# Moving 128 rows of the second dense matrix to 64 partitions, and splitting the bias, x and last output-weight transfers

## The chip, the core and the metric

The kernel runs on one core of a Trainium2 chip. A time is the device time of one execution in microseconds (us); the figure for a kernel is the median over several executions. Beside it there is one profiled execution, taken by the hardware profiler, with a time of its own.

## The reference, cut to what matters

There are two batch rows of one token each, with 448 features. A layer norm of x feeds two branches, and the output is x plus both.

```python
xn = _layernorm(x)                       # x: [2, 1, 448], bf16
# branch A: decode attention, 16 query heads on 8 key/value heads, head size 256
q = (xn @ wq)                            # wq: [448, 4096]
k, v = last 4096 positions of k_cache, v_cache   # [2, 8, 32768, 256]
p = softmax(q k^T / 16)
a = (p v) @ wo                           # wo: [4096, 448]
# branch B: a dense layer, an activation, a dense layer
h = xn @ w1 + b1                         # w1: [448, 1792], b1: [1792]
act = h * tanh(log1p(exp(h)))            # "mish"
b = act @ w2                             # w2: [1792, 448]
out = x + a + b
```

The keys and values that are read come to 67 MB; wq and wo are 3.7 MB each, w1 and w2 are 1.6 MB each. All of it is read once.

## The kernel before, in words

The order of every engine's instructions is the order of the program text (`tc.manual_schedule()`); the framework adds the waits. All large loads are issued by SyncE (SP) on one hardware queue, and ScalarE (ACT) issues x and the bias on another. Every DMA is cut over the core's 16 DMA engines, and each of these works through its own share of the queue in order.

Large loads go into a ring of three buffers (`kv`, bufs=3) of 32 KB per partition. In order of the program these are: K of step 0 first half (L98), wq (L132), K second half, w1 (L502), and then, for each step u, K of the next step, V of this step, K second half, V second half (L106), and the output weights `wo` of the step (L113). In the last step V comes in pieces, the output weights in two transfers (L119), and w2 in four parts (L556). A load waits until the buffer's earlier contents have been used. A DMA's completion is counted on one of eight semaphores, given out in turn to the DMAs of both queues, so that a DMA is also not issued before the one eight places earlier has landed.

The 8 key/value heads are worked on in four steps u of two heads each. In a step VectorE (DVE) transposes K in SBUF (`turns`, L271, two instructions for each half), TensorE (PE) computes the scores (`scores`, L358), ACT takes the exponential (L366), DVE transposes the result into `p` (L369) and swaps parts of it (L338 to L340), PE sums the weights (`weigh`, L382) and multiplies them with V (`values`, L404). `gather` (L416, L422), `finish` (L449) and `relay` (L463, L474) bring the head outputs into shape, and `mix_early` (L483) multiplies them with `wo` into one PSUM tile, `early`, which holds x from the start (L231). In the last step `carry` moves `early` to the accumulator `acc` (L238, L240), and `values_fixed` (L437), `mix` and `dense_out` (both through `add_rows`, L251) add to `acc`; DVE and ACT copy `acc` to the result (L619, L621), and SP stores it (L622).

Branch B: `dense_in` (L513) computes h for the 1792 hidden features with 49 matmuls as soon as w1 is there, `mish` (L527 to L545, with the bias from L128) turns it into `act_bf`, both in step 0. `dense_out` multiplies it with w2 at the very end. The hidden features are held as two halves k of 896; in each half, partition p has the seven features 7p to 7p+6, and so row 7p+i of the half of w2 lies on partition p at place i:

```python
w2_parts = ((0, 0, NI), (1, 0, 4), (1, 4, 6), (1, 6, NI))   # half, first place, last place; NI = 7
```

Of the kernel before, what the change touches and what calls it, by code (L numbers as in the profile page):

```python
# [11 lines left out]
BF16 = mybir.dt.bfloat16  # L12
FP32 = mybir.dt.float32
# [4 lines left out]
def kernel(  # L18
# [13 lines left out]
    nc = tc.nc  # L32
    P = 128
# [5 lines left out]
    Bsz, Sq, D = A_x.shape  # L39
    _, Hkv, Sk, Dh = A_k_cache.shape  # L40
    HqDh = A_wq.shape[1]
    Hq = HqDh // Dh
    rep = Hq // Hkv
# [4 lines left out]
    U = Hkv // KU  # L48
# [9 lines left out]
    NS = 7  # L58
    HW = HqDh // 2
    NCH = HW // P  # L60
    F2 = F // 2
    NI = F2 // P
# [6 lines left out]

    lead_pool = ctx.enter_context(tc.tile_pool(name="lead", bufs=1))  # L70
    lead_pool.tile([P, 192], BF16, name="lead")
    kv_pool = ctx.enter_context(tc.tile_pool(name="kv", bufs=3))
    kt_pool = ctx.enter_context(tc.tile_pool(name="kt", bufs=1))
    wo_pool = ctx.enter_context(tc.tile_pool(name="wo", bufs=2))
    p_pool = ctx.enter_context(tc.tile_pool(name="pp", bufs=1))
    consts = ctx.enter_context(tc.tile_pool(name="consts", bufs=1))
# [7 lines left out]
    ps_m = ctx.enter_context(tc.tile_pool(name="ps_m", bufs=1, space=PSUM))  # L84
# [5 lines left out]
    def ring(name):  # L90
        return kv_pool.tile([P, RK * KE], BF16, tag="kv", name=name)
# [3 lines left out]
    def load_k(u, r):  # L95
        t = ring("k")
        src = kview[u][:, s0:, :].rearrange("j (c t) d -> c j (t d)", c=C)
        nc.sync.dma_start(out=t[:], in_=src[:, :, r * RK * KE : (r + 1) * RK * KE])  # L98
        k_t[u, r] = t

    def load_v(u, g, lo=0, hi=TV):
        if lo == 0:
            v_t[u, g] = ring("v")
        t = v_t[u, g]
        src = vview[u][:, s0:, :].rearrange("j (g x t) d -> g x j (t d)", g=GV, x=C)
        nc.sync.dma_start(  # L106
            out=t[:, lo * Dh : hi * Dh], in_=src[g, :, :, lo * Dh : hi * Dh]
        )

    def load_wo(u):  # L110
        w = wo_pool.tile([P, KU, rep, 2 * D], BF16, tag="wo", name="wo")
        if u < U - 1:
            nc.sync.dma_start(  # L113
                out=w[:].rearrange("p k h e -> p (k h e)"),
                in_=A_wo.rearrange("(k u y i) d -> u y k (i d)", k=KU, u=U, i=8)[u],
            )
        for k2 in range(KU if u == U - 1 else 0):
            r0 = (u + U * k2) * rep * Dh
            nc.sync.dma_start(  # L119
                out=w[:, k2, :, :],  # L120
                in_=A_wo[r0 : r0 + rep * Dh, :].rearrange("(h p c) d -> p h (c d)", h=rep, p=P),
            )
        wo_t[u] = w

    x_bf = consts.tile([Bsz, D], BF16)
    nc.scalar.dma_start(out=x_bf[:, :], in_=A_x.flatten_outer_dims())
    b1_sb = consts.tile([P, 2, NI], BF16)
    nc.scalar.dma_start(out=b1_sb[:], in_=B_b1.rearrange("(k q c) -> q k c", k=2, q=P))  # L128

    load_k(0, 0)  # L130
    wq = ring("wq")
# [1 line left out]
        out=wq[:, 0 : NS * HW], in_=A_wq.flatten().rearrange("(p e) -> p e", p=P)  # L133
# [4 lines left out]
    ident = consts.tile([P, P], BF16)  # L138
# [9 lines left out]
    for k in range(KU):  # L148
        nc.gpsimd.tensor_copy(
            out=hot[:, k, :, :, :, k],  # L150
            in_=ident[:].rearrange("p (q y) -> p y q", y=4).unsqueeze(2)
            .to_broadcast([P, 4, rep, 32]),
        )
    eps_t = consts.tile([Bsz, 1], FP32)
    nc.vector.memset(eps_t[:], 1e-5)
# [7 lines left out]
        out=rstd[:], in_=mv[:, 1:2], func=ACT.Sqrt, bias=eps_t[:], scale=1.0  # L163
# [4 lines left out]
        out=xn_bf[:],  # L168
# [8 lines left out]
        out=parm[:], in_=ident[:].rearrange("p (a o) -> p o a", o=2), axis=AXIS.X, op=ALU.add  # L177
# [3 lines left out]
        out=jm[:],  # L181
        in_=ident[:].rearrange("p (a j h) -> p j a h", j=J, h=rep),
# [4 lines left out]
        out=jm[:], in0=jm[:], scalar1=-1.0, scalar2=29952.0, op0=ALU.add, op1=ALU.mult  # L187
# [3 lines left out]
        out=mneg[:], in_=jm[:].unsqueeze(1).to_broadcast([P, TH * 8, J])  # L191
    )
    sel = consts.tile([P, 2, NQ], FP32)
    for x in range(2):
        for w in range(4):
            at = 32 * w + (2 * (w % 2) + x) * NQ
            src = ident[:, at : at + NQ]
            if w == 0:
                nc.vector.tensor_copy(out=sel[:, x, :], in_=src)
            else:  # L200
                nc.vector.tensor_tensor(
                    out=sel[:, x, :], in0=sel[:, x, :], in1=src, op=ALU.add
# [16 lines left out]
    for odd in range(2):  # L219
        for half in range(2):  # L220
            o = (half + odd) % 2
            nc.vector.tensor_scalar(
                out=xs[:, odd::2, half * Bsz : (half + 1) * Bsz],
# [6 lines left out]
    early = ps_e.tile([Bsz, D], FP32)  # L230
# [18 lines left out]
    def add_rows(lhsT, rows, stop=False):  # L249
        for g in range(G):  # L250
            nc.tensor.matmul(  # L251
                acc[32 * g : 32 * g + Bsz, :],
                lhsT=lhsT,
                rhs=rows[:, g * DG : (g + 1) * DG],
                start=False,
                stop=stop,
                skip_group_check=True,
            )
# [9 lines left out]
    def turns(u, i):  # L268
        t = k_t.pop((u, i))
        for r in range(RK):  # L270
            nc.vector.transpose(  # L271
                out=kt[i][:, :, r, :, :],
                in_=t[:, r * KE : (r + 1) * KE].bitcast(FP32).rearrange(
                    "p (a c j) -> p a c j", c=P // (R * J), j=J
                ),
            )

    spread = {}
    for n in range(2):
        for e in range(2):  # L280
# [3 lines left out]
                out=sp[:],  # L284
                in_=ident[:, o : o + 63 : 2].unsqueeze(1).to_broadcast([P, G, 32]),
# [91 lines left out]
    state = {}  # L377

    def weigh(u):
        dn = ps_den.tile([P, G * TH, NQ], FP32, tag="dn", name="dn")  # L380
        for i in range(NH):
            nc.tensor.matmul(  # L382
                dn[:].rearrange("p a q -> p (a q)"),
                lhsT=ones[:],
                rhs=p_run[:, i].rearrange("p t q -> p (t q)"),
                start=(i == 0),
                stop=(i == NH - 1),
            )
        rec = small.tile([P, NQ], FP32, tag="rec", name="rec")
        nc.vector.tensor_reduce(  # L390
            out=rec[:], in_=dn[:].rearrange("p a q -> p q a"), axis=AXIS.X, op=ALU.add
        )
        nc.vector.reciprocal(out=rec[:], in_=rec[:])
        state["rec", u] = rec
# [84 lines left out]
    def mix_early(u):  # L479
        ox = state.pop(("ox", u))  # L480
        w = wo_t.pop(u)[:].rearrange("p k h (c d) -> p (k h c) d", c=2)
        for i in range(8):
            nc.tensor.matmul(  # L483
                early[:],
                lhsT=ox[:, i, :],
                rhs=w[:, i, :],
                start=False,
                stop=(u == U - 2 and i == 7),
            )
# [8 lines left out]
    act_bf = consts.tile([P, NI, 2, Bsz], BF16)  # L498

    def load_w1():  # L500
        t = ring("w1")
        nc.sync.dma_start(  # L502
            out=t[:, 0 : NS * F2], in_=B_w1.flatten().rearrange("(p e) -> p e", p=P)
        )
        state["w1"] = t

    def dense_in():
        w1 = state.pop("w1")
        w1_v = w1[:, 0 : NS * F2].rearrange("p (s q i) -> p s i q", s=NS, i=NI)
        h_ps = ps_m.tile([P, NI, 2, Bsz], FP32, tag="m", name="h_ps")  # L510
        for i in range(NI):
            for s in range(NS):
                nc.tensor.matmul(  # L513
                    h_ps[:, i, :, :].rearrange("p k b -> p (k b)"),
                    lhsT=w1_v[:, s, i, :],
                    rhs=xs[:, s, 0 : 2 * Bsz],
                    start=(s == 0),
                    stop=(s == NS - 1),
                    skip_group_check=True,
                )  # L520
        state["h"] = h_ps
# [23 lines left out]
        nc.vector.tensor_tensor(out=act_bf[:], in0=h_sb[:], in1=t_sb[:], op=ALU.mult)  # L545

    KH = 4096
    w2_parts = ((0, 0, NI), (1, 0, 4), (1, 4, 6), (1, 6, NI))

    def load_w2(part):  # L550
        if part == 0:
            state["w2"] = ring("w2")
        k, lo, hi = w2_parts[part]
        w2_in = B_w2.flatten().rearrange("(k p e) -> k p e", k=2, p=P)
        at = k * KH
        nc.sync.dma_start(  # L556
            out=state["w2"][:, at + lo * D : at + hi * D],
            in_=w2_in[k, :, lo * D : hi * D],
        )

    def dense_out(part):
        k, lo, hi = w2_parts[part]
        for i in range(lo, hi):
            at = k * KH + i * D
            add_rows(
                act_bf[:, i, k, :], state["w2"][:, at : at + D], stop=(k == 1 and i == NI - 1)
            )

    load_w1()
    turns(0, 0)  # L570
    project()
    scores(0, 0)
# [2 lines left out]
    mish()  # L575
    scores(0, 1)
    weigh(0)
    for u in range(U - 1):
        load_k(u + 1, 0)
        load_v(u, 0)  # L580
        load_k(u + 1, 1)
        load_v(u, 1)
        load_wo(u)
        turns(u + 1, 0)
        values(u, 0)
        scores(u + 1, 0)
        turns(u + 1, 1)
        values(u, 1)
        gather(u)
        finish(u)  # L590
        scores(u + 1, 1)
        weigh(u + 1)
        relay(u)
        mix_early(u)
    u = U - 1
# [19 lines left out]
    for g in range(G):  # L615
        dst = res[:, g * DG : (g + 1) * DG]
        src = acc[32 * g : 32 * g + Bsz, :]
# [35 lines left out]
```

## Time and profile before

| | |
|---|---|
| median of 6 runs | 189.43 us (189.29 to 189.69) |
| profiled execution, its own time | 190.85 us |
| its span, first to last instruction | 189.1 us |
| PE busy | 85.0 us (45%), 845 matmuls |
| DVE busy | 93.0 us (49%) |
| ACT busy, POOL busy | 12.8 us (7%), 4.7 us (2%) |
| DMA | 77.78 MB in 4719 packets, 411 GB/s over the span |
| mean granted PE clock | 0.667 |

A row of the profile gives the engine, the source line (L271 is line 271 of the kernel), the operation, the tile written and the tiles read, and how often it ran. "PE" is a matmul and "PEld" the load of its weights. A row that begins with SPq or ACTq is the issue of a DMA by that engine's sequencer, not the transfer. "Waits" name the engine and line that waited, and what ended the wait. The "chain that ended last" is followed backwards from the last instruction, at each step to what released it; a DMA in it counts from issue to landing, the time in the queue included.

### The profile page before, as it was taken

How to read it: one execution, taken by the hardware profiler on the slowest of the kernel's cores; microseconds unless marked ns; L12 is line 12 of the kernel's file. 1: busy time of each engine (PE TensorE's matmuls, PEld its weight loads, DVE VectorE, ACT ScalarE, POOL GpSimd, SP SyncE). 2: the span in 40 equal slices, each digit the busy share in tenths (PEclk: the TensorE clock that was granted, in tenths of full speed). 3: DMA queues.
4: the chain of work that ended last, by engine and by line, in shares of the span. 5: the costliest groups of instructions: out<-in, count | busy, mean ns of one | idle time of the engine just before them, and what ended most of it. 6: DMA issues, size and time to landing. Idle time of an engine off the chain costs nothing.

```text
span 189.1 us, 1937 instructions
## 1 busy us (share of the span) xinstructions
PE 85.0 (45%) x845; PEld 36.7 (19%) x849; DVE 93.0 (49%) x93; ACT 12.8 (7%) x26; POOL 4.7 (2%) x16
## 2 busy tenths in 40 slices
PE   0300357563129001892656004874383007838874
PEld 0100112520013000441122001412021002503363
DVE  6729634974891197005990493017960890041001
ACT  3000031001000100101001000110001000110111
POOL 8100000000000000000000000000000000000000
PEclk9999996755556955555578855555769755555585
DMA  5999999999999989999999999999999999999970
GB/s 222 444 416 407 446 437 408 444 440 444 444 444 444 413 383 456 417 430 430 437 444 433 444 444 416 444 444 437 419 402 430 430 416 444 444 419 401 421 318 1
DMA packets 4719, 77.78 MB, mean 411 GB/s; under 512 B 740, under 2 KB 1512, under 8 KB 2280
## 3 DMA queue, kind: packets, MB, share of 16 engines
q1 hardware_dynamic: 4436, 77.66, 96.0%
q8 instruction: 6, 0.10, 0.2%
q10 hardware_dynamic: 276, 0.01, 0.1%
q14 instruction: 1, 0.01, 0.0%
HBM read 77.67 MB, written 0.00 MB: 411 GB/s over the span
## 4 chain that ended last, share of the span: by engine, by line
DMA 43%; PE 25%; DVE 22%; issue 3%; ACT 3%; another core or an unknown queue 1%; SPq 1%; DVEq 0%; ACTq 0%
DMA v<-in_A_v_cache_dram 27%; DVE kt L271 16%; DMA k<-in_A_k_cache_dram 16%; PE pv L404 8%; PE sc L358 8%; PE o L422 4%; DVE p L369 3%; PE early L483 2%; ACT ex L366 1%; ACT vs L416 1%; PE acc L251 1%; DVE rec L390 1%; PE o L437 1%; PE dn L382 1%
## 5 line engine op out<-in xcount | busy, mean ns | idle before, releaser
L271 DVE STREAM_TRANSPOSE kt<-k 128x4096 f32<-128x4096 f32 x16 | 70.0, 4415 | 30.0 <-DMA k<-in_A_k_cache_dram 30.0
L404 PE MATMUL pv<-v,p 128*32 128x512 bf16 x240 | 25.0, 591 | 56.0 <-DMA v<-in_A_v_cache_dram 56.0
L358 PE MATMUL sc<-kt,qd 128*32 128x512 bf16 x256 | 24.6, 537 | 3.3 <-DVE qd L326 1.6
L404 PEld LDWEIGHTS <-p 128*32 128x32 bf16 x240 | 8.9, 133 | 70.5 <-issue 60.7
L449 DVE TENSOR_TENSOR oT<-o,rec 128x16 bf16<-128x16 f32 x4 | 0.7, 175 | 33.0 <-PE o L422 21.2
L369 DVE STREAM_TRANSPOSE p<-ex 128x512 bf16<-128x512 bf16 x8 | 5.2, 690 | 15.9 <-ACT ex L366 15.9
L358 PEld LDWEIGHTS <-qd 128*32 128x32 bf16 x256 | 7.8, 120 | 17.0 <-issue 13.3
L483 PE MATMUL early<-wo,ox 128*2 128x448 bf16 x24 | 9.4, 572 | 1.3 <-ACT ox L474 1.3
L366 ACT ACTIVATE ex<-sc 128x512 bf16<-128x512 f32 x8 | 4.8, 597 | 68.9 <-PE sc L358 43.9
L293 PE MATMUL q_ps<-wq,xs 128*32 128x512 bf16 x28 | 3.2, 629 | 13.3 <-DMA wq<-in_A_wq_dram 13.3
L382 PE MATMUL dn<-p,ones 128*128 128x512 bf16 x5 | 2.8, 607 | 12.0 <-DVE p L340 12.0
L422 PE MATMUL o<-sel,vs 128*128 128x8 f32 x32 | 6.7, 339 | 2.8 <-ACT vs L416 2.8
L422 PEld LDWEIGHTS o<-sel,vs 128*128 128x128 f32 x32 | 6.4, 293 | 6.0 <-ACT vs L416 6.0
L416 ACT COPY vs<-pv 128x512 f32<-128x512 f32 x4 | 2.3, 586 | 54.8 <-PE pv L404 54.8
L390 DVE TENSOR_REDUCE rec<-dn 128x8 f32<-128x512 f32 x4 | 2.8, 692 | 4.5 <-remote 3.4
L214 PE MATMUL xr_ps<-ident,xrows 2*128 2x2 bf16 x7 | 1.0, 181 | 7.2 <-DVE xrows L213 7.2
L513 PE MATMUL h_ps<-xs,w 128*128 128x4 bf16 x49 | 2.8, 193 | 2.7 <-DMA w<-in_B_w_dram 2.7
L293 PEld LDWEIGHTS <-xs 128*32 128x32 bf16 x28 | 1.1, 136 | 14.9 <-issue 14.9
L347 PE MATMUL sc<-mneg,ident 128*128 128x512 bf16 x7 | 3.9, 563 | 0.0
L483 PEld LDWEIGHTS <-ox 128*2 128x2 bf16 x24 | 2.5, 115 | 6.0 <-issue 4.4
L382 PEld LDWEIGHTS <-ones 128*128 128x128 bf16 x8 | 0.6, 110 | 15.5 <-DVE p L340 11.7
L513 PEld LDWEIGHTS <-w 128*128 128x128 bf16 x49 | 2.7, 154 | 3.6 <-DMA w<-in_B_w_dram 3.6
(65 smaller groups left out, 42.4 us busy)
## 6 DMA issues: line engine op xcount, KB each, us to landing
k<-in_A_k_cache_dram SPq DMA_DIRECT2D x8, 4096.0 KB, 27.5
v<-in_A_v_cache_dram SPq DMA_DIRECT2D x7, 4096.0 KB, 19.9
wq<-in_A_wq_dram SPq DMA_DIRECT2D x1, 3584.0 KB, 20.3
wo<-in_A_wo_dram SPq DMA_DIRECT2D x3, 896.0 KB, 18.8
v<-in_A_v_cache_dram SPq DMA_DIRECT2D x1, 2048.0 KB, 17.7
w<-in_B_w_dram SPq DMA_DIRECT2D x1, 1568.0 KB, 13.1
v<-in_A_v_cache_dram SPq DMA_DIRECT2D x1, 1536.0 KB, 21.8
wo<-in_A_wo_dram SPq DMA_DIRECT2D x2, 448.0 KB
```

What stands on the lines that cost most here:

```text
L271: nc.vector.transpose(out=kt[i][:, :, r, :, :], in_=t[:, r * KE : (r + 1) * KE].bitcast(FP32).rearrange("p (a c j) -> p a c j", c=P // (R ...
L293: nc.tensor.matmul(q_ps[32 * u : 32 * (u + 1), :], lhsT=xs[:, s, :], rhs=wq_t[s][:, u * 512 : (u + 1) * 512], start=(s == 0), stop=(s == N ...
L358: nc.tensor.matmul(sc[32 * w : 32 * (w + 1)].rearrange("p t c m -> p t (c m)"), lhsT=qd[:, u, 2 * n + e, :, :].rearrange("p g q -> p (g q) ...
L366: nc.scalar.activation(out=ex[:, :, :, i, :], in_=sc[:], func=ACT.Exp, scale=scale)
L369: nc.vector.transpose(out=p_all[:, :, h * TH : (h + 1) * TH, :].rearrange("p g t q -> p t g q"), in_=ex[:, h * TH : (h + 1) * TH].rearrang ...
L382: nc.tensor.matmul(dn[:].rearrange("p a q -> p (a q)"), lhsT=ones[:], rhs=p_run[:, i].rearrange("p t q -> p (t q)"), start=(i == 0), stop= ...
L390: nc.vector.tensor_reduce(out=rec[:], in_=dn[:].rearrange("p a q -> p q a"), axis=AXIS.X, op=ALU.add)
L404: nc.tensor.matmul(pv[32 * w : 32 * (w + 1), :, :].rearrange("p x d -> p (x d)"), lhsT=p_run[:, g, 4 * a : 4 * a + 4, :].rearrange("p t q ...
L416: nc.scalar.copy(out=sb[:].rearrange("p x d -> p (x d)"), in_=pv[:].rearrange("p x d -> p (x d)"))
L422: nc.tensor.matmul(po[:, c, :], lhsT=sb[:, x, c::2], rhs=sel[:, x, :], start=(x == 0 and c == 0), stop=(last and x == 1), skip_group_check ...
L483: nc.tensor.matmul(early[:], lhsT=ox[:, i, :], rhs=w[:, i, :], start=False, stop=(u == U - 2 and i == 7),)
L513: nc.tensor.matmul(h_ps[:, i, :, :].rearrange("p k b -> p (k b)"), lhsT=w1_v[:, s, i, :], rhs=xs[:, s, 0 : 2 * Bsz], start=(s == 0), stop= ...
```

## The change

**w2.** In each half, the first 128 features are now one to a partition (place 0), and the other 768 are six to a partition (places 1 to 6). `dense_in` takes its weight columns accordingly. Place 0 of the second half, 128 rows of w2, is not in the ring any more: it has a tile of its own, `w2_low`, on partitions 0 to 63 with two rows each, filled by two transfers of 32 partitions right after w1. For it, `dense_out_low` brings the 128 activations into the order of these 64 partitions with two small matmuls (by `perm`, made on POOL) and a copy on DVE, and then adds two matmuls of 448 columns to `early`, in step 0 behind `weigh(0)`. `dense_out` at the end has 13 places in place of 14, in another order of parts.

**Transfers.** The bias comes in four transfers in place of one, x in two, and the output weights of the last step in four in place of two. A pad tile `lead2` is added.

```diff
+    w2_low = lead_pool.tile([P // 2, 2, D], BF16, name="w2_low")
+    lead_pool.tile([P, 128], BF16, name="lead2")
...
         for k2 in range(KU if u == U - 1 else 0):
-            r0 = (u + U * k2) * rep * Dh
-            nc.sync.dma_start(
-                out=w[:, k2, :, :],
-                in_=A_wo[r0 : r0 + rep * Dh, :].rearrange("(h p c) d -> p h (c d)", h=rep, p=P),
-            )
+            for h in range(rep):
+                r0 = ((u + U * k2) * rep + h) * Dh
+                nc.sync.dma_start(
+                    out=w[:, k2, h, :],
+                    in_=A_wo[r0 : r0 + Dh, :].rearrange("(p c) d -> p (c d)", p=P),
+                )
...
-    nc.scalar.dma_start(out=x_bf[:, :], in_=A_x.flatten_outer_dims())
+    for b in range(Bsz):
+        nc.scalar.dma_start(out=x_bf[b : b + 1, :], in_=A_x.flatten_outer_dims()[b : b + 1, :])
     b1_sb = consts.tile([P, 2, NI], BF16)
-    nc.scalar.dma_start(out=b1_sb[:], in_=B_b1.rearrange("(k q c) -> q k c", k=2, q=P))
+    b1_in = B_b1.rearrange("(k f) -> k f", k=2)
+    b1_top = b1_in[:, 0:P].rearrange("k (q c) -> q k c", c=1)
+    b1_low = b1_in[:, P:].rearrange("k (q c) -> q k c", q=P)
+    nc.scalar.dma_start(out=b1_sb[:, :, 0:1], in_=b1_top)
+    for lo, hi in ((0, 48), (48, 96), (96, P)):
+        nc.scalar.dma_start(out=b1_sb[lo:hi, :, 1:NI], in_=b1_low[lo:hi])
...
+    perm = consts.tile([P, 2, 2, 8, 4], BF16)
+    for j in range(2):
+        nc.gpsimd.tensor_copy(
+            out=perm[:, j],
+            in_=ident[:, j::2].rearrange("p (z b a) -> p z a b", z=2, b=4),
+        )
...
-        w1_v = w1[:, 0 : NS * F2].rearrange("p (s q i) -> p s i q", s=NS, i=NI)
+        w1_v = w1[:, 0 : NS * F2].rearrange("p (s f) -> p s f", s=NS)
...
-                    lhsT=w1_v[:, s, i, :],
+                    lhsT=w1_v[:, s, 0:P] if i == 0 else w1_v[:, s, P + i - 1 :: NI - 1],
...
-    w2_parts = ((0, 0, NI), (1, 0, 4), (1, 4, 6), (1, 6, NI))
+    w2_parts = ((0, 1, NI), (1, 1, 5), (1, 5, NI), (0, 0, 1))
+    def w2_at(k, i):
+        return k * KH + (i - 1) * D if i > 0 else 2 * KH
+
+    act_low = consts.tile([P // 2, 2, Bsz], BF16)
+
+    def load_w2_low():
+        rows = B_w2[F2 : F2 + P, :].rearrange("(z b a j) d -> z a b (j d)", z=2, b=4, a=8)
+        for z in range(2):
+            nc.sync.dma_start(
+                out=w2_low[32 * z : 32 * (z + 1)].rearrange("p j d -> p (j d)"), in_=rows[z]
+            )
+
+    def dense_out_low():
+        ap_ps = ps_m.tile([P // 2, 2, Bsz], FP32, tag="m", name="ap_ps")
+        for j in range(2):
+            nc.tensor.matmul(
+                ap_ps[:, j, :],
+                lhsT=perm[:, j].rearrange("p z a b -> p (z a b)"),
+                rhs=act_bf[:, 0, 1, :],
+                start=(j == 0),
+                stop=(j == 1),
+                skip_group_check=True,
+            )
+        nc.vector.tensor_copy(out=act_low[:], in_=ap_ps[:])
+        for j in range(2):
+            nc.tensor.matmul(
+                early[:], lhsT=act_low[:, j, :], rhs=w2_low[:, j, :], start=False, stop=False
+            )
 
     def load_w2(part):
         if part == 0:
             state["w2"] = ring("w2")
         k, lo, hi = w2_parts[part]
-        w2_in = B_w2.flatten().rearrange("(k p e) -> k p e", k=2, p=P)
-        at = k * KH
-        nc.sync.dma_start(
-            out=state["w2"][:, at + lo * D : at + hi * D],
-            in_=w2_in[k, :, lo * D : hi * D],
-        )
+        rows = B_w2[k * F2 : (k + 1) * F2, :]
+        if lo == 0:
+            src = rows[0:P, :]
+        else:
+            src = rows[P:, :].rearrange("(p i) d -> p (i d)", p=P)[:, (lo - 1) * D : (hi - 1) * D]
+        at = w2_at(k, lo)
+        nc.sync.dma_start(out=state["w2"][:, at : at + (hi - lo) * D], in_=src)
...
     load_w1()
+    load_w2_low()
     turns(0, 0)
...
     weigh(0)
+    dense_out_low()
     for u in range(U - 1):
```

More of the change, by code (lines that the diff above doesn't have):

```diff
@@ L563, in dense_out @@
         for i in range(lo, hi):
-            at = k * KH + i * D
+            at = w2_at(k, i)
             add_rows(
-                act_bf[:, i, k, :], state["w2"][:, at : at + D], stop=(k == 1 and i == NI - 1)
+                act_bf[:, i, k, :], state["w2"][:, at : at + D], stop=(part == len(w2_parts) - 1)
             )
     load_w1()
+    load_w2_low()
     turns(0, 0)
```

## The prediction

> **What bounds the kernel now.** I read the DMA rows of the page first, then the chain that ended last, then the timeline of the end, then the trace's packet and semaphore records, which the views only sum up. The page says the DMA engines are never idle:
>
> ```profile
> DMA  5999999999999989999999999999999999999970
> ...
> q1 hardware_dynamic: 4436, 77.66, 96.0%
> q8 instruction: 6, 0.10, 0.2%
> q10 hardware_dynamic: 276, 0.01, 0.1%
> ```
>
> q1 is SP's queue, q10 ACT's (x and the bias), q8 the fetch of instructions. The reader is to see the 96.0% and the flat row of nines: a byte more in the queue is time for whatever stands behind it. The chain (start, us, what), cut to its last third, says which load that hits:
>
> ```profile
> 131.38 8.65 DVE kt L271 x2
> 140.03 0.02 issue
> 140.05 16.95 DMA v<-in_A_v_cache_dram
> 157.00 0.04 issue
> 157.04 3.63 PE pv L404 x32
> ...
> 169.84 0.29 DVE p L340
> ...
> 176.21 4.21 PE pv L404 x48
> ...
> 184.19 2.26 PE acc L251 x46
> 186.45 0.25 DVE res L619
> ```
>
> After 157.04 no DMA is in the chain: 30 us of PE, ACT and DVE work run to the end without waiting for a load. So the end is the landing of v(2,1), the last V half of step 2, plus a fixed tail. Its 16.95 us are mostly queue: issued at 140.05, its first packet starts at 145.13 in the packet records, 5.1 us later. A free queue took 2.149 - 0.733 = 1.4 us from issue to first packet (the first K load), so an issue may come some 3.7 us later at no cost. The other loads of the three loop steps have more.
>
> The sixteen engines do not finish v(2,1) together. Its semaphore arrivals are eleven at 155.17 to 155.59, one at 156.11, four at 156.68, 156.72, 156.96 and 157.00. The four agree with four instruction packets before it (16384 B, at 39.26, 63.52, 101.05, 135.75): each takes 0.88 to 0.94 us on one engine and stretches its next 32 KB packet from 1.21 to about 1.75, some 1.43 us together, never made up; each arrival group gains one late member after such a packet. The 156.11 is a table load at 69.56 that cost half a us. **The chain waits for the four late engines.** The profile doesn't number them; that is the main unknown.
>
> **w2_low, the load.** It adds two transfers behind w1, each four packets of 1792 B on engines 0 to 7, and a semaphore packet. Such packets follow each other at 1.137 us for 16 and a semaphore (wo at 171.50 to 172.64), 0.071 each: 2 x (4 x 0.071 + 0.006) = 0.58 us on engines 0 to 7, none on 8 to 15. All of it stands before v(2,1) in the queue. If the late four are among 8 to 15, the other half goes from at most 155.59 to 156.2 (156.7 for the table load's engine), still before 157.00: cost nothing. If one of the last two is among 0 to 7, v(2,1) lands 0.58 later; if only the 156.7 pair is, about 0.3. I take nothing, because the load is confined to half the engines and has 1.4 us of cover there, and keep 0.58 as the other end. SP issues the two at 22.4 to 23.5, where it idles until 25.07; by those rows the issue is free.
>
> The row on independence: engines stand 1.8 us apart at 155.17 and 157.00 and none waits for another. The Trainium skill speaks against the change here (SBUF — State Buffer, "Door 1: The DMA port swizzle"): 64 partitions reach only 8 of 16 ports, about half the bandwidth. By that rule, if the queue as a whole waited for the slow transfer, everything behind it would move by an estimated 0.5 us and the sum below would read about 189.9; the arrivals above speak for charging engines 0 to 7 alone.
>
> **w2, the rest.** Each engine loses eight packets of 896 B at the end: w2's last part took 182.23 to 182.54 on the first engine, 0.31 us. It lies behind v(2,1), and PE doesn't wait for w2: the last landing is 184.72, PE gets to its last four matmuls at about 186.2, so no gain. On PE, `dense_out` drops from 56 to 52 matmuls, and these are on the path:
>
> ```profile
> 160.69 13.51 SPq L556 DMA_DIRECT2D w<-in_B_w_dram  x4
> 184.89 1.52 PE L251 MATMUL acc<-w,act_bf 128*2 128x112 bf16 x56
> ```
>
> 1.52 / 56 = 0.027; four fewer is -0.11 us.
>
> **dense_out_low.** PE: two small matmuls and two of 448 columns (0.572 each by L483), 1.3 us, between the end of `dn` at 47.9 and PE's next work at 55.71, when v(0,0) has landed: hidden. DVE: one copy of 64x4 from PSUM, 0.2 us by L449's 0.175, ahead of `turns(1,0)`. This moves the issue of v(0,1) from 57.48 to 57.7; its first packet starts at 63.37, 4.5 us of cover after 1.4 of latency. Without cover it would cost 0.2 in the loop. POOL: two copies of 64 columns, at most 0.43 each (0.85 for two of 256), before the memset of xs, which DVE needs at 8.26: hidden.
>
> **Bias and x.** ACT issues six DMAs at 0.43 to 0.53 us in place of two: 1.9 us later to its table load and the square root. x's second row is issued at about 1.26, where the bias was issued at 1.29, whose first packet got through at 5.07: ACT's queue gets a turn only after each of SP's packets. So x is complete at 5 to 7 in place of 2.0, and the norm's DVE work (6.8 us from L158 to the end of L222, other constants included) ends at 12 to 13.9 in place of 8.9. K is transposed from 13.21, so up to 0.7 later; that costs w1's issue 0.7 of the 8.6 us before its first packet (22.01 to 30.60), and q has until wq at 21.86. Hidden.
>
> The bias had 16 packets and a semaphore per engine, and took 17 turns, 5.07 to 21.37. Now it has 16 + 6 + 6 + 4 and four semaphores, 36, plus x's: 38 turns at most. Behind SP's packets (7 + 1 of K, 8 + 1 of wq, K, w1 each) that is 35 turns at 34.8 and the last by 38.6, on an engine without w2_low. `mish` needs it here:
>
> ```profile
> 40.23 0.19 DVE L527 TENSOR_TENSOR h_sb<-h_ps,b_sb 128x28 f32<-128x28 f32 x1
> ```
>
> It fits by 1.3 us; behind L527 on DVE stand only `mish` and, at 44.51, L369, so 2.6 us more are free there, then 4.5 us in the queue. As load, 19 to 21 more packets per engine at 4 ns (K packets follow each other at 1.213 us with a bias packet between them, at 1.209 to 1.210 without): +0.08 us on every engine, and on the path, for all of it is before v(2,1).
>
> **wo in four.** The same bytes, two more semaphore packets behind v(2,1), two more issues on SP (1.10 us for two) at 156.72, and behind them V's last pieces and w2. A DMA waits for the one eight places earlier; so the first w2 part now waits for v(3,0), 169.13, and the last for a quarter of wo, about 174.9; the queue reaches w2 at 178.68. Hidden; V's last pieces are issued by 160 and start at 173.77. `dense_in` with stride 6 for 7 stays between 35.17 and K's transpose at 40.2.
>
> **Sum.** +0.08 (bias packets) - 0.11 (four matmuls) + 0 = -0.03 us on the profiled execution's 190.85, that is 190.82. The median is 1.42 lower (189.43); the same difference gives 189.4.
>
> **Rivals.** *Late engines among 0 to 7* (slower). For it: sixteen engines, and no row says which half got the instruction packets. Against it: the packets come to a different engine each time, in a sequence, so that four in a row can well lie in one half. Price 0.58, from the point where one of the last two engines carries w2_low: 190.0. Chance 0.33.
>
> *SP is held by the bias* (slower). Two w2 issues waited for V pieces:
>
> ```profile
> SPq L556 <- DMA v<-in_A_v_cache_dram: 4.3, 2, 2.9
> ```
>
> They went at 169.14 and 173.86, just behind the landing of the DMA eight places earlier (169.13, 173.84). With six more DMAs in the round, K of step 1 (issue 25.07) waits for a bias transfer. If it is the first one, landing at about 24, nothing happens; if it is the last, the issue comes at about 35 and the queue runs dry at 34.8 for the 1.4 us of latency: some 1.5 us, 190.9. In the round of before, ACT's and SP's DMAs alternate, which makes it the first. Chance 0.07.
>
> *A better start* (faster). The first K packets start at 2.15 to 3.04 and end at 3.87 to 4.33; this spread of 0.46 is still there at 155.17 to 155.59, and two of the four late engines are at its late end. The bias, 256 pieces, was issued into that moment; now x's few pieces are. If that made the spread, v(2,1) gains up to 0.4; with the sum above, 189.0. Against it: the early starters needed 1.7 to 2.0 us for a packet that later takes 1.21, so the memory may set it. Chance 0.20.
>
> That w2_low is spread over all engines would cost 0.29, inside the range. The forecast has the remaining 0.40.
>
> **How the numbers follow.** 0.2% is 0.38 us, about what a measurement of this kernel can tell from no change. Faster: 0.15 from the better start and 0.05 from the forecast's own scatter. Slower: 0.27 from the late engines, 0.07 from the bias, 0.03 scatter. The rest is within. The range goes from the better start, 189.0, to the late engines with 0.2 of scatter, 190.2; it leaves out the held queue and thin tails.
>
> **What would show it.** Right: the landing of v(2,1) in the chain stays at 157.0 +- 0.2, the `acc` matmuls of `dense_out` are 52 in 1.41 us, no DMA in the chain behind v(2,1), L527 still right behind the transposes at 40.2. Wrong: that landing at 157.6 (late engines), a gap in the DMA row near 35 us (the bias), a landing before 156.7 (the start), or a w2 wait in front of L251.

## The result, and the profile after

The changed kernel takes **190.93 us** (median of 31 runs, 190.51 to 192.72) against 189.45 us for the kernel before on the same chip (66 runs): ratio 1.0080 [1.0064, 1.0096]. It is slower by 1.5 us; the prediction said 189.4 us in 189.0 to 190.2. About a quarter of the executions of either kernel are some 1.5 us longer than the rest, and the profiled execution that the prediction worked on, 190.85 us, is one of those; the profiled execution of the changed kernel, 190.89 us (span 189.1 us), is one of its usual ones. So these two profiles, equal in time, are not a fair pair, and a second profile of the kernel before was taken: **189.42 us, span 187.6 us**. It is "the usual execution of before" below.

The page of the changed kernel (DMA rows):

```profile
DMA  6999999999999999999999999999999999999991
...
DMA packets 5135, 77.78 MB, mean 411 GB/s; under 512 B 1092, under 2 KB 1928, under 8 KB 2696
...
q1 hardware_dynamic: 4548, 77.66, 96.5%
q8 instruction: 6, 0.10, 0.2%
q10 hardware_dynamic: 580, 0.01, 0.2%
```

q10, the queue of x and the bias, has 580 packets in place of 276 for the same 0.01 MB. By share of time it still seems to be nothing.

The chain of waits of the changed kernel (start, us, what), its end:

```profile
121.62 27.45 DMA k<-in_A_k_cache_dram
...
157.89 17.52 DMA v<-in_A_v_cache_dram
175.42 9.88 DMA w<-in_B_w_dram
...
185.35 0.54 PE acc L266 x16
185.89 0.01 issue
185.91 0.60 PE acc L266 x12
186.50 0.25 DVE res L665
```

And of the usual execution of before:

```profile
136.80 20.26 DMA v<-in_A_v_cache_dram
157.06 0.04 issue
157.10 3.63 PE pv L404 x25
160.73 0.02 issue
160.75 0.35 SPq L556
161.09 0.04 issue
161.13 22.71 DMA w<-in_B_w_dram
183.85 0.04 issue
183.89 1.13 PE acc L251 x27
185.02 0.25 DVE res L619
```

The 30 us of compute that ended the chain in the prediction are in neither. Both chains come to the end through a part of w2: it is awaited at 183.85 before and at 185.31 after, and everything behind it is equal (1.13 and 1.14 us on PE, one copy, the store). The difference, 1.46 us, is the result. Where it arises is read from windows early in the run. The columns are the window, its length, busy us and count of PE, PEld, DVE, ACT and POOL, the PE clock, the DMA share and GB/s; in 12.60 to 21.30 us q1 holds mostly wq, and q10 the bias. The window counts a packet where it starts, so a row can be off by some packets (the profile on record of before reads 448). The usual execution of before, then after:

```profile
12.60:21.30 8.70, 0.00 (x0) 0.00 (x0) 8.02 (x2) 0.00 (x0) 0.00 (x0) 1.00 1.01 432
```

```profile
12.60:21.30 8.70, 0.00 (x0) 0.00 (x0) 7.82 (x2) 0.00 (x0) 0.00 (x0) 1.00 1.01 402
```

The engines are as busy (1.01 both) but move less. With the bytes of each packet in the packet records spread over its time, the rates are 430 GB/s before and 383 after; 47 GB/s over 8.7 us are 0.41 MB, 0.95 us at 430. In the same records the last end of each early load shows the same, cumulated:

| load, last packet ends at (us) | before, usual execution | after | later by |
|---|---|---|---|
| K, first half | 12.91 | 13.15 | 0.24 |
| wq | 21.44 | 22.64 | 1.20 |
| K, second half | 31.13 | 32.45 | 1.32 |
| w1 | 34.86 | 36.24 | 1.38 |
| last landing of w2 | 184.68 | 186.16 | 1.48 |

The time is lost by 36 us, most of it beside wq, and never made up.

### The profile page after: what moved, and what is told of

It reads as the page before. It is cut to its first block, busy times and chain, and to the rows that moved or that the text cites. A ratio compares the mean times of both kernels' runs of the same rounds, so it can differ in the third digit from the quotient of the medians.

```text
span 189.1 us, 1951 instructions
## 1 busy us (share of the span) xinstructions
PE 74.4 (39%) x845; PEld 32.7 (17%) x849; DVE 93.6 (49%) x94; ACT 12.8 (7%) x26; POOL 5.1 (3%) x18
## 4 chain that ended last, share of the span: by engine, by line
DMA 68%; DVE 17%; PE 9%; issue 3%; ACT 1%; ACTq 0%; another core or an unknown queue 0%; DVEq 0%
DMA v<-in_A_v_cache_dram 29%; DMA k<-in_A_k_cache_dram 15%; DVE kt L286 14%; DMA b_sb<-in_B_b_dram 12%; DMA w_low<-in_B_w_dram 7%; DMA w<-in_B_w_dram 5%; PE pv L419 4%; PE sc L373 3%; DVE p L384 1%; DVE rec L405 1%; ACT ex L381 1%; PE acc L266 1%; PE o L437 1%; PE dn L397 1%; ACTq L130 0%
## 5 line engine op out<-in xcount | busy, mean ns | idle before, releaser
L286 DVE STREAM_TRANSPOSE kt<-k 128x4096 f32<-128x4096 f32 x16 | 70.0, 4416 | 33.7 <-DMA k<-in_A_k_cache_dram 33.7
L419 PE MATMUL pv<-v,p 128*32 128x512 bf16 x240 | 23.9, 571 | 61.2 <-DMA v<-in_A_v_cache_dram 61.2
L373 PE MATMUL sc<-kt,qd 128*32 128x512 bf16 x256 | 19.1, 436 | 3.8 <-DVE kt L286 1.9
L498 PE MATMUL early<-wo,ox 128*2 128x448 bf16 x24 | 8.7, 538 | 1.3 <-ACT ox L489 1.3
L373 PEld LDWEIGHTS <-qd 128*32 128x32 bf16 x256 | 6.8, 103 | 13.3 <-issue 7.3
L397 PE MATMUL dn<-p,ones 128*128 128x512 bf16 x5 | 2.2, 477 | 12.0 <-DVE p L355 12.0
L437 PE MATMUL o<-sel,vs 128*128 128x8 f32 x32 | 4.4, 265 | 2.8 <-ACT vs L431 2.8
L437 PEld LDWEIGHTS o<-sel,vs 128*128 128x128 f32 x32 | 4.1, 196 | 6.0 <-ACT vs L431 6.0
L528 PE MATMUL h_ps<-xs,w 128*128 128x4 bf16 x49 | 2.3, 184 | 3.1 <-DMA w<-in_B_w_dram 3.1
L528 PEld LDWEIGHTS <-w 128*128 128x128 bf16 x49 | 2.2, 138 | 3.8 <-DMA w<-in_B_w_dram 3.8
```

The lines of the kernel that those rows point to most:

```text
L286: nc.vector.transpose(out=kt[i][:, :, r, :, :], in_=t[:, r * KE : (r + 1) * KE].bitcast(FP32).rearrange("p (a c j) -> p a c j", c=P // (R ...
L373: nc.tensor.matmul(sc[32 * w : 32 * (w + 1)].rearrange("p t c m -> p t (c m)"), lhsT=qd[:, u, 2 * n + e, :, :].rearrange("p g q -> p (g q) ...
L397: nc.tensor.matmul(dn[:].rearrange("p a q -> p (a q)"), lhsT=ones[:], rhs=p_run[:, i].rearrange("p t q -> p (t q)"), start=(i == 0), stop= ...
L419: nc.tensor.matmul(pv[32 * w : 32 * (w + 1), :, :].rearrange("p x d -> p (x d)"), lhsT=p_run[:, g, 4 * a : 4 * a + 4, :].rearrange("p t q ...
L437: nc.tensor.matmul(po[:, c, :], lhsT=sb[:, x, c::2], rhs=sel[:, x, :], start=(x == 0 and c == 0), stop=(last and x == 1), skip_group_check ...
L498: nc.tensor.matmul(early[:], lhsT=ox[:, i, :], rhs=w[:, i, :], start=False, stop=(u == U - 2 and i == 7),)
```

## The experiments

**Theories.** *Pieces*: the 256 two-byte pieces of the first bias transfer slow the large packets beside them (wq's packets take 1137 ns on average, 1062 ns before). *Halves*: w2_low delays the late engines (the prediction's main rival). *Issue*: SP is held by the bias. Within *pieces*, what counts could be the number of transfers, the size of a piece, or where its source lies. In the table, "usual" is the median of the executions that are not of the long kind (189.4 for the kernel before beside every one). Ratios and intervals are over all runs but one (223.12 us, of e10_top_last's four), so they carry the share of long ones: two of e14_same's four, none of e9_after_rows' ten, about a quarter to two fifths of those of before.

| kernel | usual us | ratio | wq packet, ns | wq ends, us |
|---|---|---|---|---|
| after | 190.92 | 1.0080 [1.0064, 1.0096] | 1137 | 22.64 |
| e1_before | 189.39 | 1.0012 [0.9984, 1.0041] | 1062 | 21.47 |
| e2_bias4 | 191.01 | 1.0072 [1.0042, 1.0103] | 1141 | 22.66 |
| e3_bias1 | 189.60 | 0.9997 [0.9959, 1.0035] | 1062 | 21.57 |
| e4_low | 189.54 | 1.0006 [0.9977, 1.0035] | 1062 | 21.37 |
| e5_top12 | 189.94 | 1.0015 [0.9979, 1.0050] | 1062 | 21.46 |
| e6_top4 | 190.53 | 1.0054 [1.0015, 1.0094] | 1108 | 22.02 |
| e7_spread | 189.80 | 1.0004 [0.9965, 1.0043] | 1062 | 21.45 |
| e8_rows | 189.28 | 1.0003 [0.9964, 1.0042] | 1062 | 21.34 |
| e9_after_rows | 189.68 | 0.9983 [0.9954, 1.0012] | 1062 | 21.31 |
| e10_top_last | 190.93 | 1.0076 [1.0058, 1.0094] | 1062 | 21.58 |
| e11_x2wo4 | 189.73 | 1.0019 [0.9986, 1.0052] | 1062 | 21.41 |
| e12_low_rows | 189.54 | 0.9997 [0.9972, 1.0022] | 1062 | 21.36 |
| e13_far | 189.70 | 1.0003 [0.9973, 1.0033] | 1062 | 21.42 |
| e14_same | 190.94 | 1.0112 [1.0048, 1.0175] | 1139 | 22.67 |
| e15_x2 | 189.62 | 1.0018 [0.9984, 1.0052] | 1062 | 21.40 |

### Which part of the change: e1, e2, e3, e4

**e1_before** is the kernel before, unchanged.

> The kernel before, unchanged, for a profile in its usual state: the profile on record took 190.85 us against a median of 189.45, while the changed kernel's profile (190.89) stands at its own median. Theory A (the bias in four transfers slows the first loads, and the usual execution is bound by DMA to its end): the new profile is about 189.4, and a DMA stands in its chain within the last 5 us, in front of the last acc matmuls, with the last w2 landing at about 184.7 and PE done at once behind it. Theory B (128 rows on engines 0 to 7 hold the late engines): no statement on the tail; the chain could end in PE work as in the profile on record.

Its times are those of before. It was run to profile a usual execution, but the profiled one, 190.89 us, is of the long kind. Its chain ends as the one on record, without a DMA:

```profile
182.32 1.66 PE o L437 x64
...
184.23 2.26 PE acc L251 x71
```

**e2_bias4**: before, with the new four bias transfers (the b1 lines of the diff) and nothing else, so that the bias reaches other features. **e3_bias1**: the change with the old single transfer, `nc.scalar.dma_start(out=b1_sb[:], in_=B_b1.rearrange("(k q c) -> q k c", k=2, q=P))`. **e4_low**: before with the w2 part alone.

> The kernel before with nothing changed but the bias: four transfers, 256 pieces of 2 bytes and 256 of 12 in place of 256 of 14 (the biases then stand at other hidden features than in the reference). Theory A: 190.7 to 190.9 us, wq lands at about 23.0 in place of 21.9 and the second K half at about 32.9 in place of 31.4. Theory B: 189.4 to 189.6, wq at 21.9 and K at 31.4 to 31.6.

> The changed kernel with the bias in one transfer as before (so that the biases stand at other hidden features), all else of the change kept: x in two, w2_low, output weights in four. Theory A: 189.3 to 189.6 us, wq lands at 21.9. Theory B: 190.7 to 190.9, as the changed kernel, wq at 21.9 and the loss behind w1.

> The changed kernel with only the w2 part left: bias in one transfer (biases at other features), x in one, output weights in two. Theory A: 189.2 to 189.6 us; engines 0 to 7 carry 0.58 us more at the front and all carry 0.31 less at the end, so the last landing differs from the kernel before by -0.3 to +0.3. Theory B: 189.9 to 190.9.

The bias alone brings the whole loss (191.01) and taking it out removes nearly all of it (189.60). The chain of e2_bias4 has the form of the usual one of before, 1.25 us later (of its 1.6 us, 0.2 more lie behind the store, see "What is left over" below):

```profile
162.37 22.73 DMA w<-in_B_w_dram
185.10 0.04 issue
185.14 0.54 PE acc L256 x16
```

e4_low ends at 189.54, with nothing gained and nothing lost that the interval shows.

### What about the bias: e5, e6, e7, e13, e14

All five are the kernel before with four bias transfers, of which the last three are those of the change (e13_far: the same pieces from another place). They differ in the first, and each has 256 pieces in it; the bias values are other ones, or go to other features.

```diff
 e5_top12   # 12 bytes each, sources 12 bytes apart, into a tile that nothing reads
+    nc.scalar.dma_start(out=b1_x[:], in_=b1_low)
 e6_top4    # 4 bytes each, sources 4 bytes apart, into a tile that nothing reads
+    nc.scalar.dma_start(out=b1_x[:], in_=b1_in[:, 0 : 2 * P].rearrange("k (q c) -> q k c", c=2))
 e7_spread  # 2 bytes each, sources 14 bytes apart
+    nc.scalar.dma_start(out=b1_sb[:, :, 0:1], in_=b1_all[:, :, 0:1])
 e13_far    # 2 bytes each, sources at least 1.8 KB apart; the other three likewise from w1
+    b1_far = B_w1[0:P, :].rearrange("q (k f) -> q k f", k=2)
+    nc.scalar.dma_start(out=b1_sb[:, :, 0:1], in_=b1_far[:, :, 0:1])
 e14_same   # 2 bytes each, for each half k all from one element
+    b1_same = b1_in[:, 0:1].rearrange("k (q c) -> q k c", c=1).to_broadcast([P, 2, 1])
+    nc.scalar.dma_start(out=b1_sb[:, :, 0:1], in_=b1_same)
```

> The kernel before with four bias transfers, but the first one has 256 pieces of 12 bytes (into a spare tile) in place of 256 of 2 bytes; place 0 of the bias is zero and the others stand at other features. Theory A1 (pieces of 2 bytes are what is dear): 189.4 to 189.6 us, wq packets at 1.062 us and wq's last packet ends at 21.5. Theory A2 (the number of pieces, or the four transfers, are dear): 190.8 to 191.0, wq packets at 1.14 and wq's end at 22.6, as with the bias in four.

> As the one before, but the first transfer has 256 pieces of 4 bytes. Theory A1, the 2-byte size alone: 189.4 to 189.6. If the loss goes with the share of a small memory region that all engines read at the same time (256 pieces out of 1 KB here, out of 512 bytes with the 2-byte pieces): 190.3 to 190.9. If any piece under 8 bytes is dear: 190.9.

> The kernel before with four bias transfers, the first with 256 pieces of 2 bytes, but their sources lie 14 bytes apart, as the pieces of the kernel before do, in place of 2 bytes apart (place 0 of the bias is then right, the others stand at other features). Theory A1 (size): 190.8 to 191.0, as with the bias in four. Theory A3 (all engines read the same few bytes of memory): 189.5 to 189.9.

> The kernel before with the four bias transfers in the same shapes and sizes (256 pieces of 2 bytes, 256 of 12), but read from w1, at sources 1.8 KB and more apart, in place of the bias (so the biases are other numbers). If closeness of the sources is the whole cost: 189.3 to 189.5 us, wq's end at 21.4 and the second K half at 31.1. If the number of pieces costs the 0.4 us that were left with sources 12 or 14 bytes apart: 189.8 to 190.0 and K at 31.35.

> The kernel before with four bias transfers, of which the first reads the same element 128 times for each half (place 0 of the bias is then one number for each half, the others stand at other features). If closeness of the sources is the cost: at least that of sources 2 bytes apart, 191.0 to 191.6 us, wq packets at 1.14 us or more. If it is the many different short reads in a row, and one element is served from a buffer: 189.8 to 190.0, wq packets at 1.062.

e7_spread and e14_same read as many pieces, of the same size, into the same places, and differ in the sources alone. The same window as above, e7_spread first:

```profile
12.60:21.30 8.70, 0.00 (x0) 0.00 (x0) 8.03 (x2) 0.00 (x0) 0.00 (x0) 1.00 1.07 458
```

```profile
12.60:21.30 8.70, 0.00 (x0) 0.00 (x0) 7.54 (x2) 0.00 (x0) 0.00 (x0) 1.00 1.00 396
```

458 against 396 GB/s by this view, 430 against 389 with the packets spread over their times; wq is done at 21.45 against 22.67. So what delays wq is neither the number of transfers, nor the number of packets, nor their size, but that many pieces read the same few bytes: side by side (e2_bias4) is as bad as one element (e14_same), 4 bytes apart delays wq by about half as much (22.02), 12 or 14 bytes apart not at all. The pieces' own records hide this: a two-byte packet takes about 9 ns in both, like the 14-byte ones of before. The cost stands in the rows of the large packets beside them: 75 to 79 ns on each of wq's eight packets, 0.6 us, and longer gaps between them, 0.2 to 0.3 us in all.

The Trainium skill (DMA: Bandwidth & Descriptors, "Why small descriptors are slow (HBM only)") prices a small descriptor by a fixed overhead, some three cycles and 32 bytes. By that, e7_spread and e14_same would cost the same; they differ by 1.1 us. The same page ("How a descriptor splits into AXI transactions") says that reads are made from 256-byte-aligned addresses; by an estimate from this, pieces 2, 4 and 14 bytes apart share such a block 128, 64 and some 18 at a time, which is the order of the losses. No run here shows that these blocks are the reason.

What is left over: e5, e7 and e13 stay 0.3 to 0.5 us above the kernel before with wq on time. Of this, 0.23 us lie at the very end. From the last landing of the result's store to the end of the span it is 0.83 to 0.84 us in all three profiles of before, and 1.06 us in these three, as in every profiled kernel with 35 transfers. It goes with the number of transfers, not with the loads: 32 (before, e8_rows) 0.83 to 0.84, 33 (e15_x2) 0.93, 34 (e4, e12) 1.00, 35 (e2, e5, e6, e7, e10, e11, e13, e14) 1.06 to 1.07, 37 (e3, e9) 1.02, and with the 40 of the changed kernel 0.84 again. Why is open; 32 and 40 are whole rounds of the eight semaphores. The rest is 0.0 to 0.3 us. In e5_top12 K's second half already ends 0.26 us later than in the usual execution of before, in e13_far 0.03; the cause of this rest is open.

### Does the place in the run matter: e10

```diff
     for lo, hi in ((0, 48), (48, 96), (96, P)):
         nc.scalar.dma_start(out=b1_sb[lo:hi, :, 1:NI], in_=b1_low[lo:hi])
+    nc.scalar.dma_start(out=b1_sb[:, :, 0:1], in_=b1_top)
```

The four bias transfers of e2_bias4 with the two-byte pieces last; then they run beside K's second half and w1 and not beside wq.

> The kernel before with the four bias transfers in another order: the three of 12-byte pieces first, the 2-byte pieces last, so that they run beside the second K half and w1 in place of the first K half and wq (biases at other features). If the stretch belongs to the 2-byte pieces whatever runs beside them: 190.8 to 191.1 us, wq's end at 21.5 and the second K half about 1 us late. If it needs wq beside them: 189.5 to 190.0.

The loss moves with the pieces and keeps its size: 190.93 (three usual runs). The two windows around the change of place, e10_top_last:

```profile
12.60:21.30 8.70, 0.00 (x0) 0.00 (x0) 7.88 (x2) 0.00 (x0) 0.00 (x0) 1.00 1.06 453
...
31.00:36.00 5.00, 1.56 (x16) 0.34 (x8) 4.16 (x1) 0.60 (x1) 0.00 (x0) 0.83 1.12 426
```

and e1_before in the second:

```profile
31.00:36.00 5.00, 2.06 (x30) 0.91 (x19) 4.51 (x2) 0.60 (x1) 0.00 (x0) 0.80 1.13 487
```

wq is back at 453 GB/s; between 31 and 36 us the rate falls from 487 to 426, and w1 ends at 35.98 against 34.89. By the view alone the second reading would be weak, for e2_bias4, whose two-byte pieces are over by then, also shows 426 there. With the packets spread over their times it is 356 GB/s in e10_top_last, 426 in e2_bias4 and 431 in e1_before, and w1's packets take 533 ns in place of 469. In both places the loss falls on the weights: beside K's second half the two-byte pieces cost no more than other small ones (its packets take 1232 ns, 1243 in e5_top12 with 12-byte pieces, 1213 in e1_before). Why is not shown; in both places the weights are also beside the later half of the pieces.

### Without the pieces: e8, e9, e12

The bias as two rows of 1792 bytes, two packets in place of 256, which PE adds with seven small matmuls into `h_ps`; e8_rows on the kernel before, e9_after_rows on the whole change, e12_low_rows on e4_low.

```diff
+    b1_row = consts.tile([2, F2], BF16)
+    nc.scalar.dma_start(out=b1_row[:], in_=B_b1.rearrange("(k f) -> k f", k=2))
...
+            nc.tensor.matmul(h_ps[:, i, :, :].rearrange("p k b -> p (k b)"),
+                lhsT=b1_row[:].rearrange("k (q c) -> k c q", c=NI)[:, i, :],
+                rhs=bsel[:].rearrange("p k b -> p (k b)"), start=False, stop=True, ...)
```

> The kernel before with the bias as two pieces of 1792 bytes, on two partitions, added to h by seven small matmuls in front of the activation; no small pieces are left. If all small pieces on ACT's queue cost the loads behind them: 189.1 to 189.4 us, that is up to 0.3 less than before, wq's end at 21.3 to 21.4. If the 14-byte pieces cost nothing: 189.45 +- 0.1.

> The whole change, but with the bias as two pieces of 1792 bytes that are added to h by seven small matmuls; the result is the reference's. Theory A (the 2-byte pieces with sources side by side are the whole loss): 189.2 to 189.7 us, wq's last packet ends at 21.3 to 21.5 in place of 22.6. Theory B (another part of the change costs as well): 190 or more.

> The w2 part of the change alone (x in one, output weights in two) with the bias as two pieces added by matmuls; the result is the reference's. With the tail bound by the w2 landings, which came 0.28 earlier with the w2 part (183.45 in place of 183.73): 189.0 to 189.3 us. If the end is not bound by w2: 189.4 to 189.5.

With rows the whole change costs nothing that the interval shows: 0.9983 [0.9954, 1.0012]. That interval is helped by the lack of long runs among the ten; the usual runs stand 0.28 us above before, 0.19 of them behind the store (1.02 us in place of 0.83). Of e8_rows and e12_low_rows neither is shown to be faster than before; the lowest, e8_rows, has its w2 wait at 183.73 (183.85 before):

```profile
160.99 22.74 DMA w<-in_B_w_dram
183.73 0.04 issue
183.77 0.54 PE acc L255 x16
```

### The small parts: e11, e15

**e11_x2wo4**: before with x in two and the output weights in four transfers; **e15_x2**: x alone.

> The kernel before with x in two transfers and the last output weights in four, nothing else. By the prediction's steps both are hidden: 189.4 to 189.55 us. If they explain the 0.16 us between the kernel without the bias split (189.73) and the one with the w2 part alone (189.57): 189.6 to 189.7.

> The kernel before with x in two transfers and nothing else. With x in two and the output weights in four the usual runs rose by 0.3 us (189.73 against 189.42). If x costs it, by starting the first K load worse: 189.7, first K half at 13.0 or later. If the output weights cost it, by issuing w2 later: 189.4.

Both stand 0.2 to 0.3 us above before with intervals that include 1, and 0.10 us of e15_x2's and 0.23 us of e11_x2wo4's excess lie behind the store; the parts are cheap, and these runs don't tell them from free. There is no better start: K's first half ends at 12.87 in e15_x2, 12.91 before.

### A usual profile of before: e16

**e16_before** is the kernel before, unchanged, profiled once more.

> The unchanged kernel, one look. If the look falls on a usual execution (about 189.4 us): a w2 landing stands in the chain in front of the last acc matmuls, as in the kernel with the bias in rows (landing at 183.73 there), and PE's clock is above 0.7. If it takes 190.9 again: the chain ends in PE work, as in the two profiles on record.

189.42 us; its chain is shown above. Why the profile on record had another end is seen in the windows of its last third. Before on record:

```profile
160.00:170.00 10.00, 6.49 (x49) 2.85 (x41) 2.21 (x6) 1.18 (x2) 0.00 (x0) 0.50 0.95 406
170.00:180.00 10.00, 8.49 (x72) 3.09 (x74) 1.02 (x3) 0.86 (x3) 0.00 (x0) 0.54 1.01 417
```

e16_before:

```profile
160.00:170.00 10.00, 5.82 (x62) 2.71 (x56) 3.23 (x8) 1.52 (x4) 0.00 (x0) 0.84 0.94 401
170.00:180.00 10.00, 6.35 (x83) 3.06 (x82) 0.00 (x0) 1.11 (x2) 0.00 (x0) 0.84 1.01 418
```

The DMA columns agree. PE was granted 0.50 to 0.54 of its clock on record and 0.84 here, and on record it is busy 8.49 of 10 us in the second window (8.43 also in e8_rows, a usual execution, at a clock of 0.67). In both, w2 lands for the last time at the same moment, 184.72 and 184.68; on record PE came to it 1.5 us late.

## Why the prediction was wrong, by its own steps

**The step that failed is "As load, 19 to 21 more packets per engine at 4 ns": +0.08 us.** It measured some 1.5 us: in the changed kernel w2 is awaited 1.46 us later, and e2_bias4, with the bias alone, takes 191.01 against 189.4. It priced the packets by the gap that a 14-byte bias packet makes between two packets of K. That is a price for pieces whose sources lie 14 bytes apart, and e7_spread shows that nothing is lost on wq there; the new pieces lie two bytes apart. About 1.2 us come from that (191.01 against 189.80, with the same number of transfers). Some 0.2 us more are what e7_spread still loses without its 0.23 us behind the store, which the changed kernel doesn't have. I bounded this cost from one row only, and a row of the right kind did not exist in the trace.

**"After 157.04 no DMA is in the chain" and "PE doesn't wait for w2"** held for the profile on record and not for a usual execution, where PE stands 0.27 us idle for w2 until 183.89; in the changed kernel, too, the w2 wait that the prediction named as a sign of being wrong stands in front of `acc`. From the timeline of e16_before (in brackets what PE waited for):

```profile
183.89 1.09 PE L251 MATMUL acc<-w,act_bf 128*2 128x112 bf16 x28 [0.27 <-DMA w<-in_B_w_dram]
```

The 1.42 us between profile and median was carried through the sum as a constant; it was the mark of another bound. The profile told it: the last landing of w2 at 184.72, and PE there at 186.2, are 1.5 us apart, nearly those 1.42 us. For the loss of 1.5 us itself the bound matters little, since all of it was before v(2,1), which the chains of e16_before and e2_bias4 both pass (at 157.06 and 158.20). For "no gain" of the w2 part and the 0.11 us of four matmuls it was the wrong frame.

**Late engines.** Four engines were late, as read. Whether they carry w2_low differs between the profiles: in e4_low and e3_bias1 v(2,1) lands at 156.91 and 156.93, as before (157.06), in e12_low_rows at 157.25, in e9_after_rows at 157.47, and in the changed kernel at 158.73, 0.53 after e2_bias4. The arrivals fit: in e4_low the last four come at 156.78 to 156.90 as before, and seven others at 155.71 to 156.18 in place of 155.14 to 155.66. So both the forecast and the rival of 0.58 us were seen. Each of these is one profile; whether the kernel or the execution decides it is not settled. At the end each engine has 0.26 us of w2 less to load (eight packets of 5376 B in place of 6272 B; the prediction counted eight packets fewer, 0.31 us), and the last landing of w2 is 184.29 in e4_low and 184.93 in e9_after_rows (184.68 before): on the whole free, as the sum had it, but by balance and not by cover.

**SP held by the bias** came true, and cost nothing. K of step 1 was issued at 32.82 us in place of 25.07, for it waited for the second bias transfer. The waits of SP in the changed kernel (engine, line, waited for: total us, times, longest):

```profile
SPq L100 <- DMA b_sb<-in_B_b_dram: 7.7, 1, 7.7
```

The queue did not run dry: w1 had packets until 36.24, made later by the loss itself, and those of K follow without a gap. The second w2_low transfer was held as well, until the first bias transfer landed at 24.29. The head of the changed kernel's chain names these two (12.0% and 6.6% of the span):

```profile
1.53 22.76 DMA b_sb<-in_B_b_dram
24.29 0.02 issue
24.31 12.54 DMA w_low<-in_B_w_dram
36.84 0.49 issue
37.34 4.42 DVE kt L286
```

This is a false lead: by the timeline the two transposes of which L286 at 37.34 is the second run without a pause from 32.97 on, released by K. The rival's 190.9 us is the measured time, by another cause.

**Hidden, as said.** x complete at 5.6 us (said: 5 to 7), the last bias transfer at 36.77 (by 38.6), `mish` right behind the transposes, and `dense_out_low` in a gap of PE. From the timeline of the changed kernel (start, us, what; in brackets what its engine waited for):

```profile
41.77 0.19 DVE L542 TENSOR_TENSOR h_sb<-h_ps,b_sb 128x28 f32<-128x28 f32 x1
...
49.32 0.27 PE L579 MATMUL ap_ps<-act_bf,perm 128*64 128x2 bf16 x2
...
50.44 0.90 PE L589 MATMUL early<-w_low,act_low 64*2 64x448 bf16 x2 [0.85 <-DVE act_low L587]
```

**A better start** did not come (e15_x2).

## What to carry to other kernels

Where the DMA queue is the bound, price a small transfer by the large packets that run beside it, not by its own packets, and look at where its sources lie: hundreds of pieces from the same few bytes cost here 1.2 us, the same pieces 14 bytes apart none of it. A contiguous row that PE adds avoids them. Before working from a profile, compare its time with the median: where they differ by more than the runs' scatter, find what in that execution accounts for it, or the chain may name the wrong bound.

## What the runs showed that I had not expected

- A two-byte packet takes about 9 ns in the records wherever its source lies, and yet 256 of them made wq's 28 KB packets 7% longer (1062 to 1137 to 1141 ns) when the sources lay within 256 bytes for each half, and when they were one element; not when they lay 14 bytes apart.
- Whether the engines that are late carry w2_low differs between profiles (e4_low, e9_after_rows). Three of the kernels with w2_low and without the two-byte pieces, e4, e9 and e12, scatter over 0.74 to 0.87 us in their usual runs, e5, e7 and e13 over 0.18 to 0.27; but e3_bias1, also of the first kind, over 0.45, and before over 0.49. That the scatter comes from the late engines is not shown.
- The time behind the last store, 0.83 to 1.07 us, goes with the number of transfers in the whole kernel; two kernels that are compared at 0.2 us should have it equal.
- The executions that are some 1.5 us longer: three profiles of them (before, e1_before, e13_far) show a PE clock of 0.51 to 0.54 between 170 and 180 us, and the usual ones 0.59 to 0.84 (e16_before, e2_bias4, e4_low and the changed kernel 0.84, e8_rows 0.67, e5_top12 and e9_after_rows 0.63, e6_top4 0.59). What brings the lower clock is open.
